# A long convolution by a two-stage Fourier transform beside a diagonal state-space layer, on one core: parity rows in two partition halves, spectra in one layout, and part of the shift convolution on TensorE

## The chip, the cores and the metric

The kernel runs on one core of a Trainium2 chip. The metric is the device time of one execution in microseconds (us). The core's engines work side by side, each through its own instructions in order: TensorE (PE; its weight loads are listed as PEld), VectorE (DVE), ScalarE (ACT), GpSimd (POOL) and SyncE (SP). Transfers are issued from two queues here, SP's and POOL's, and are carried by 16 shared DMA engines.

## The reference

Two independent heads over 2048 time steps and 1024 channels, written side by side into one output of 2048 rows and 2048 columns. All inputs are bf16.

```python
# head A (H3): k, v, q of [2048, 1024]; shift_k [1024, 4]; ssm_k [1024, 2048]; ssm_D [1024]
kv = (causal 4-tap convolution of k along time, with shift_k per channel) * v
y  = (causal convolution of kv along time with ssm_k per channel, by an FFT of length 4096)
a  = q * (y + kv * ssm_D)
# head B (S5): x [2048, 1024], 1024 complex states, diagonal Lam_bar
Bu   = x @ B_bar.T                        # complex
h[t] = Lam_bar * h[t-1] + Bu[t]           # 2048 steps
b    = 2 * real(h @ C.T) + x * Dskip
```

## The kernel before

**Head B** goes in 16 chunks of 128 time steps. For a chunk i, `U.i.*` (line 492) makes 128 matmuls of 128x128 weights `BT` on the transposed chunk `xT`, `ue` copies them out of PSUM on ACT (line 497), then VectorE rotates (`r1`, `r2`: lines 506 and 518), runs the recurrence as a scan (`sc`, line 523), carries the state over (`cm`), and rotates back (`r3`, `r4`: lines 506 and 535). `y.i.*` (lines 546 and 551) multiplies the states by `CT`, 32 matmuls of 512 columns and 8 small ones for the skip term, and `ye` copies that out (line 556). The weights are prepared first: `bl` loads a block of B, `bT` transposes it on TensorE (line 458), `bc` copies it into `BT` (line 473 on ACT, 469 on DVE); C and x come by transposing transfers from SP (`cx`, line 480, and `x`, line 483).

**Head A** is a transform of length 4096, split as 128 x 32. The time steps are cut into 16 residues r ("parity rows"), each a tile of 128 partitions by 1024 channels. VectorE makes kv two residues at a time: `kvm` (line 583, four products), `kva` (597) and `kvb` (602, sums), `kvc` (604, times v), from rows of k loaded by `kp` into a ring `kring`. The first stage multiplies every residue by a constant F1: `am` (line 610) for kv and `hm` (line 643) for the filter, whose transposes are `hl`, `hT` (line 630) and `hc` (635). F1 has 128 rows and 128 columns, of which half are zero, since even and odd rows share the partitions. The results are copied out (`ae` line 615, `he` line 650) and stored to DRAM (`ast`, `hst`). The second stage takes 16 groups gq: `lh` and `lk` load the stored values in another order, `sh` and `sk` (line 676) transform them in 64x64 pieces of the array, `she` (685) and `ske` (691) copy out. Real and imaginary part of a spectrum lie on different partitions; so `sw` makes a swapped copy of the filter's spectrum by four SBUF-to-SBUF transfers for each gq, and `pr` (line 704) multiplies both copies at once. `sa` (line 717) transforms back, `sae` (724) copies out and `vst` stores. The last stage `a3` (line 744) needs, for each residue r, values of all 16 groups: `vl` loads them, `a3e` (749) copies out, `qm` (753) multiplies by q (loaded by `qp`), and `ost` stores.

**Order.** A text, `ORDER`, lists every task in one sequence. Each engine runs its own tasks in that sequence; `@G` and `@S` move a transfer to POOL's or SP's queue, `@D` moves a copy to VectorE, and the letters after a colon name the buffers: `p0`, `p1` are single PSUM banks, `d0` to `d2` pairs of banks, `a` and `b` are rings in SBUF of 4 KB and 2 KB a partition. A task on TensorE that needs an occupied `p` or `d` waits for the copy that empties it.

```python
def s2(key, nm, gq, e, o): ...          # before: one half e of the channels, 64x64 pieces, one pd
def sw(gq):                             # before: four transfers of 32 partitions
    for b in range(4):
        o = b ^ 1
        spd(hab[32 * b:32 * b + 32, 1, :, :], hab[32 * o:32 * o + 32, 0, :, :])
```

Of the kernel before, what the change touches and what calls it, by code (L numbers as in the profile page):

```python
# [70 lines left out]
wb.2:p1 cx.0.1 eo.1 stt.0 wb.0:p0 cx.7.0 wbe.2 stt.1 eo.3 wb.5:p1 bl.3.0:b6 x.1:b2 wbe.5@D wbe.0 stt.3 wb.3:p1 wbe.3 bT.6.1:p0 cx.1.0 dd bT.2.0:p1
kvm.0:m0 vp.1:a1 vp.2:a0 cx.6.0 bc.6.1 cx.6.1 bT.0.1:p0 bc.2.0 bc.0.1@D kp.2@G eo.2 bT.2.1:p1 kva.0 hT.0.0:p0 hc.0.0:b8 stt.2 bc.2.1 hT.0.1:p0
bT.7.1:p1 hc.0.1:b13 kvb.0:a7 bc.7.1 hT.0.6:p0 hm.0.0.1:d0 kvc.0 hc.0.6:b10 hT.0.3:p1 hm.0.0.0:d1 kvm.4:m0 he.0.0.1:b5 am.1.1:d2 hc.0.3:b11
hm.0.6.1:d0 hst.0.0.1 hT.0.2:p0 bT.0.0:p1 he.0.6.1:b8 hc.0.2:b0 hst.0.6.1@S cx.1.1 bc.0.0 bT.7.0:p0 bc.7.0@D cx.3.1 z1 U.0.3.0:p1 kva.4 hm.0.6.0:d0
U.0.3.1 cx.3.0 U.0.2.0:p0 kvb.4:a8 U.0.2.1 ue.0.3:a10 he.0.6.0:b7 kvm.2:m0 bT.1.0:p1 bc.1.0 am.0.1:d0 bT.3.0:p1 ue.0.2 bc.3.0 bT.3.1:p0 bc.3.1
U.0.0.0:p1 U.0.0.1 he.0.0.0:b5 kp.4@G kva.2 kp.3@G ae.0.1:b10 hm.0.3.1:d1 U.2.2.0:p0 ue.0.0 ast.0.1@S vp.4:a5 kvc.4 U.0.1.0:p1 ae.1.1:b4 cx.5.0
hm.0.1.0:d0 he.0.3.1:b6 ast.1.1 kvb.2:a6 hm.0.3.0:d2 hst.0.6.0 U.0.1.1 he.0.1.0:b3 hst.0.3.1 kvc.2 U.2.2.1 ue.0.1 hst.0.1.0 he.0.3.0:b11 U.1.2.0:p1
r1.0:m0 ue.2.2:a0 hst.0.3.0@S hm.0.1.1:d1 hst.0.0.0@S am.4.0:d0 he.0.1.1:b8 cx.2.0 U.2.1.0:p0 r2.0:a1 U.1.2.1 U.2.1.1 ue.1.2:a10 kvm.8:m0 U.1.1.0:p1
ue.2.1 ae.4.0:b13 hm.0.2.0:d2 am.4.1:d1 z2 ast.4.0 am.0.0:d0 U.2.3.0:p0 hst.0.1.1 ae.4.1:b4 U.1.1.1 he.0.2.0:b7 ast.4.1@S sc.0 U.2.3.1 ue.1.1
hst.0.2.0@S hm.0.2.1:d1 cx.7.1 ue.2.3 am.5.1:d2 ae.0.0:b6 hT.0.4:p1 cx.2.1 am.2.0:d0 hc.0.4:b10 ast.0.0 U.1.0.0:p0 ae.2.0:b3 hT.0.7:p1 cx.4.0 kva.8  # L80
U.1.0.1 ue.1.0 hT.0.5:p0 hc.0.7:b0 hl.5:a9 kvb.8:a4 hl.4:a2 U.2.0.0:p1 hc.0.5:b13 ast.2.0@S hl.7:a3 r3.0:m0 U.1.3.0:p0 he.0.2.1:b8 am.1.0:d0 hst.0.2.1
hm.0.5.0:d1 U.1.3.1 cm.0:a7 kvc.8 U.2.0.1 ue.1.3 he.0.5.0:b11 r4.0 U.4.0.0:p0 ue.2.0 hm.0.4.0:d1 r1.1:m0 U.4.0.1 he.0.4.0:b5 U.4.2.0:p1 ue.4.0:a5
# [4 lines left out]
hm.1.4.1:d0 am.9.0:d2 hc.1.3:b9 hst.0.4.1@S ae.9.0:b8 hT.1.5:p0 am.9.1:d1 y.0.1.3 he.1.4.1:b5 r2.4:a5 am.3.1:d2 ye.0.1 hst.1.4.1 hm.1.3.1:d0
y.1.1.0:p1 he.1.3.1:b0 kvm.6:m0 hc.1.5:b3 y.1.1.1 hst.1.3.1@S ae.3.1:b7 hT.1.7:p0 y.1.1.2 ae.9.1:b4 hm.1.4.0:d0 hm.1.5.1:d2 hc.1.7:b10 ast.9.1 y.1.1.3
kp.6 kva.6 hT.1.6:p0 ast.9.0@S ye.1.1:b5 kp.5 hm.1.7.0:d1 hc.1.6:b13 yst.0@S y.1.0.0:p1 ast.3.1@S he.1.5.1:b0 hT.1.1:p0 cm.2:a4 kvb.6:a1 y.1.0.1
hst.1.5.1 hc.1.1:b4 lw.1@G:w0 hm.1.6.0:d2 r3.2:m0 y.1.0.2 he.1.6.0:b2 y.1.0.3 he.1.4.0:b8 hst.1.6.0@S hT.1.0:p0 r4.2 ye.1.0 hst.1.4.0 hm.1.6.1:d2  # L90
hm.1.3.0:d0 he.1.6.1:b13 vp.6@G:a6 U.3.2.0:p1 kvc.6 yst.1 he.1.7.0:b9 hst.1.6.1 hm.1.1.0:d2 kvm.12:m0 U.3.2.1 hc.1.0:b0 hst.1.7.0@S x.7:b11
hm.1.7.1:d1 y.2.0.0:p0 he.1.7.1:b10 x.6:b7 he.1.1.0:b8 y.2.0.1 hm.1.0.0:d1 hst.1.1.0@S hm.1.1.1:d2 he.1.0.0:b2 y.2.0.2 kva.12 ue.3.2:a7 am.6.1:d1
he.1.3.0:b4 U.3.3.0:p1 he.1.1.1:b9 U.3.3.1 kvb.12:a8 hst.1.1.1 hm.1.0.1:d0 ue.3.3 hst.1.0.0 ae.6.1:b5 hT.1.2:p1 kvm.10:m0 y.2.0.3 hc.1.2:b13 ast.6.1
hm.1.5.0:d2 vp.5@G:a2 am.7.0:d1 he.1.0.1:b0 hst.1.7.1 y.2.1.0:p1 ye.2.0:b8 am.7.1:d0 he.1.5.0:b3 y.2.1.1 ae.7.0:b9 kvc.12 kp.7@G hm.1.2.0:d2 y.2.1.2
hst.1.5.0 kva.10 vp.7@G:a9 U.3.1.0:p0 hst.1.3.0 hm.1.2.1:d1 U.3.1.1 he.1.2.1:b2 kvb.10:a10 y.2.1.3 he.1.2.0:b1 hst.1.2.1@S hst.1.0.1@S am.13.1:d1
lw.0:w1 ue.3.1 kvc.10 am.6.0:d2 ae.13.1:b5 U.6.0.0:p0 kvm.14:m0 ae.6.0:b10 am.10.0:d1 ast.13.1@S x.5:b13 U.6.0.1 ye.2.1 ast.6.0 am.10.1:d2 ae.7.1:b3
hst.1.2.0 U.7.3.0:p1 yst.2@S ast.7.0@S ue.6.0:a3 am.12.1:d0 ae.10.0:b2 U.7.3.1 ae.10.1:b4 U.3.0.0:p0 ast.10.0 kva.14 am.12.0:d1 ue.7.3:a6 ast.10.1@S
am.13.0:d2 U.3.0.1 U.6.3.0:p1 ue.3.0 kvb.14:a0 lh.2:a1 ae.13.0:b0 lh.0:a2 U.7.1.0:p0 lh.1:a8 r1.3:m0 ae.12.0:b5 am.11.0:d2 U.6.3.1 ae.11.0:b10
# [725 lines left out]
```

## Time and profile before

| | |
|---|---|
| device time, 3 runs | 379.9, 381.47, 382.37 us; median 381.47 |
| profiled execution, first to last instruction | 378.5 us |
| median less that span | 3.0 us |
| busy: PE, DVE, ACT, POOL | 92%, 86%, 70%, 21% of the span |
| transfers | 100.06 MB, 264 GB/s on average |

The page has the busy time of each engine, the span in 40 slices, the transfers, the chain of work that ended last, and the costliest groups of instructions (line, engine, operation, output <- inputs, shapes, count; busy time and mean length of one; idle time before them and what ended it). A view by stretches of time gives busy time, DMA share and rate. In the chain of work, a row is the start, the length, and what ran. In the view in order of time, a row is the start, the length, the engine, the line, and what was merged. The time of a single matmul in such a row includes the tail in which it drains; the distance between two starts is what it costs.

### The profile page before, as it was taken

The numbers are of one execution on the slowest core, as the hardware profiler recorded it, in microseconds if no ns is written. First come the engines' busy times: TensorE is split into PE (matmuls) and PEld (weight loads), VectorE is DVE, ScalarE is ACT, GpSimd is POOL, SyncE is SP. The second block draws the span as 40 slices with busy tenths as digits, with TensorE's granted clock in tenths as the row PEclk, the third lists the DMA queues.
The fourth block names the chain that finished last, engine by engine and source line by source line (L and its number), as shares of the span: only waits on it lengthen the run. The fifth ranks groups of instructions, "written<-read, shape, count | busy, mean of one in ns | idle before, by whom it ended". The sixth has DMA issues, their size and how long they took to land.

```text
span 378.5 us, 8748 instructions
## 1 busy us (share of the span) xinstructions
PE 346.6 (92%) x3661; PEld 225.6 (60%) x3661; DVE 324.6 (86%) x229; ACT 264.2 (70%) x341; POOL 81.3 (21%) x150
## 2 busy tenths in 40 slices
PE   4548889899899999999999999989999999999995
PEld 3226678785455578855444757367867664467442
DVE  6989599999999997999997797576899999993972
ACT  4978798877778886952785879778869771346433
POOL 7300023022112521214200325330210202211021
PEclk9999999999999999999999999999999999999999
DMA  6999999997578999999999897999989539877995
GB/s 231 317 338 216 265 272 286 296 314 235 200 243 270 247 313 287 281 272 268 190 275 312 258 324 234 220 267 221 284 236 312 175 125 325 306 229 255 350 319 206
DMA packets 67418, 100.06 MB, mean 264 GB/s; under 512 B 38435, under 2 KB 42147, under 8 KB 67380
## 3 DMA queue, kind: packets, MB, share of 16 engines
q1 hardware_dynamic: 54660, 56.32, 54.8%
q0 software_dynamic: 12720, 43.19, 36.8%
q8 instruction: 28, 0.46, 0.5%
q14 instruction: 10, 0.08, 0.1%
HBM read 49.16 MB, written 33.55 MB: 219 GB/s over the span
## 4 chain that ended last, share of the span: by engine, by line
PE 56%; DMA 15%; issue 13%; ACT 7%; SPq 4%; POOL 2%; DVE 1%; POOLq 0%; ACTq 0%; DVEq 0%
PE ps_u L492 22%; PE ps_y L546 16%; PE ps_a L744 4%; DMA wts<-a_c_W 4%; SPq L483 4%; DMA Ys_kv<-ysb 3%; PE ps_a L643 3%; DMA l2k<-Ys_kv 3%; DMA ld<-in_B_B_re_dram 3%; PE ps_a L717 3%; PE ps_a L610 3%; DMA hab<-hab 2%; PE ps_a L676 2%; PE ps_t L630 2%; ACT ysb L615 2%
## 5 line engine op out<-in xcount | busy, mean ns | idle before, releaser
L492 PEld LDWEIGHTS <-BT 128*128 128x128 bf16 x2048 | 119.3, 98 | 22.6 <-issue 11.7
L492 PE MATMUL ps_u<-xT,BT 128*128 128x128 bf16 x2048 | 127.7, 219 | 2.4 <-ACT u L497 1.2
L546 PE MATMUL ps_y<-CT,h 128*128 128x512 bf16 x512 | 127.7, 379 | 0.0
L546 PEld LDWEIGHTS <-h 128*128 128x128 bf16 x512 | 44.6, 98 | 48.0 <-issue 6.1
L523 DVE TENSOR_TENSOR_SCAN h<-rtab,h 128x2080 bf16<-128x2080 f32 x16 | 71.8, 4488 | 0.2
L497 ACT CAST u<-ps_u 128x512 bf16<-128x512 f32 x64 | 38.2, 603 | 27.0 <-PE ps_u L492 19.1
L506 DVE TENSOR_TENSOR mt<-u,Z 128x4096 bf16<-128x4096 bf16 x16 | 36.7, 2291 | 15.8 <-ACT u L497 15.4
L704 DVE TENSOR_TENSOR hab<-x,hab 128x4096 bf16<-128x4096 bf16 x16 | 36.5, 2286 | 15.2 <-DMA hab<-hab 10.5
L556 ACT CAST yo<-ps_y 128x512 bf16<-128x512 f32 x32 | 19.1, 596 | 28.0 <-PE ps_y L546 24.4
L650 ACT CAST ysbh<-ps_a 128x1024 bf16<-128x1024 f32 x32 | 32.3, 1033 | 8.8 <-PE ps_a L643 7.5
L691 ACT CAST x<-ps_a 128x1024 bf16<-128x1024 f32 x32 | 31.9, 1026 | 8.8 <-PE ps_a L676 5.9
L506 DVE TENSOR_TENSOR mt<-h,Z 128x4096 bf16<-128x4096 bf16 x16 | 36.7, 2292 | 0.5
L724 ACT CAST vsb<-ps_a 128x1024 bf16<-128x1024 f32 x32 | 31.7, 1027 | 6.5 <-PE ps_a L717 6.0
L583 DVE TENSOR_TENSOR mt<-kring,wbc 128x2048 bf16<-128x2048 bf16 (+3 forms) x14 | 35.8, 2592 | 0.4 <-ACT wbc L473 0.2
L615 ACT CAST ysb<-ps_a 128x1024 bf16<-128x1024 f32 x32 | 32.3, 1043 | 2.7 <-issue 1.6
L685 ACT CAST hab<-ps_a 128x1024 bf16<-128x1024 f32 x32 | 32.2, 1030 | 2.1 <-PE ps_a L676 1.9
L551 PE MATMUL ps_y<-Dd,xT 128*128 128x128 bf16 x128 | 28.0, 219 | 0.0
L749 ACT CAST ot<-ps_a 128x1024 bf16<-128x1024 f32 x16 | 15.7, 1018 | 14.1 <-PE ps_a L744 14.1
L169 POOL DMA_DIRECT2D Ys_h<-ysbh x20 | 14.3, 716 | 43.3 <-ACT ysbh L650 43.3
L168 POOL DMA_DIRECT2D hab<-hab x32 | 15.6, 494 | 32.1 <-ACT hab L685 18.3
L458 PE MATMUL ps_t<-ident,ld 128*128 128x128 bf16 x128 | 13.9, 285 | 9.1 <-DMA ld<-in_B_B_re_dram 4.4
L643 PE MATMUL ps_a<-hT,F1t 128*128 128x512 bf16 x64 | 20.6, 402 | 0.8 <-ACT ysbh L650 0.6
(116 smaller groups left out, 381.8 us busy)
## 6 DMA issues: line engine op xcount, KB each, us to landing
Ys_h<-ysbh POOLq DMA_DIRECT2D x20, 256.0 KB, 5.5
l2h<-Ys_h SPq DMA_DIRECT2D x9, 512.0 KB, 9.7
Vs<-vsb SPq DMA_DIRECT2D x9, 512.0 KB, 4.3
vv<-Vs SPq DMA_DIRECT2D x9, 512.0 KB, 5.2
Ys_kv<-ysb POOLq DMA_DIRECT2D x17, 256.0 KB, 6.2
l2k<-Ys_kv SPq DMA_DIRECT2D x8, 512.0 KB, 3.9
hab<-hab SPq DMA_DIRECT2D x32, 128.0 KB, 5.4
l2k<-Ys_kv POOLq DMA_DIRECT2D x8, 512.0 KB, 7.8
```

Of the source, the lines that this page charges most:

```text
L492: nc.tensor.matmul(pu[:, w, jl, :], BT[:, 2 * jp + jl, w, d, :], xT[:, d, :], start=(d == 0), stop=(d == ND - 1))
L497: nc.scalar.copy(u[:, :, 2 * jp:2 * jp + 2, :], st["pu", i, jp][:])
L506: nc.vector.tensor_mul(m, s_, w_)
L523: nc.vector.tensor_tensor_scan(gf, rtab[:].rearrange("p a j t -> p (a j t)"), gf, 0.0, ALU.mult, ALU.add)
L546: nc.tensor.matmul(py[:], h[:, 1 - w, j, 2:TP], CT[:, j, w, dh * 512:(dh + 1) * 512], start=(j == 0 and w == 0), stop=(j == NJ - 1 and w = ...
L583: nc.vector.tensor_mul(m[:, :, j0:j0 + n, :], a_, wbc[:, j0:j0 + n, :].unsqueeze(1).to_broadcast([P, 2, n, DV]))
L615: nc.scalar.copy(st["ysb", r, u][:], st["pa", r, u][:].rearrange("p e d -> p (e d)"))
L643: nc.tensor.matmul(pd[:, e, :], F1t[:, u, :], st["hT", f, rp][:, e, :], start=True, stop=not sk)
L650: nc.scalar.copy(st["yh", f, rp, u][:], st["pa", f, rp, u][:])
L685: nc.scalar.copy(hab[:, a, :, e * 512:(e + 1) * 512], st["ps", key, gq, e][:])
L691: nc.scalar.copy(x16[:, :, e * 512:(e + 1) * 512], st["ps", "k", gq, e][:])
L704: nc.vector.tensor_mul(hab, x16.unsqueeze(1).to_broadcast([P, 2, 2 * D]), hab)
```

## The change

1. **Halves.** The parity rows of k, v, q and the output lie as two halves of 64 partitions (`(n h s) d -> h n s d`), each loaded or stored by a transfer of its own: `kp`, `vp`, `qp`, `ost`, `vl` and `hst` issue two transfers where they issued one.
2. **First stage without zeros.** F1 is 64x64; `am` and `hm` make 8 matmuls of 64x64 pieces (four pieces of the array) for each residue in place of 4 of 128x128, into two pairs of banks.
3. **Last stage.** The constant G is 128x64; `a3` makes 4 matmuls in two column halves in place of 4 full ones. `hT` transposes into the same two halves: 16 pieces in place of 8.
4. **Spectra.** `sh` and `sk` make 16 matmuls of 64x32 pieces, and real and imaginary part come to lie on the same partition. `sw` and its 64 transfers are gone; `p1` and `p0`, two products of 2048 elements, replace `pr`, one of 4096. `sa` makes 32 matmuls of 32x64 pieces in place of 16 of 64x64.
5. **Shift convolution.** `NX = 2`: two of the eight blocks of 128 channels are convolved on TensorE. `kx` loads them by two transposing transfers of 2048 rows, `dg` builds diagonal weights, `kt` makes 32 matmuls of 128 columns for two residues, `ke` copies out on ACT. `kvm`, `kva` and `kvb` work on 768 channels, no longer 1024.
6. **Small ones.** The scan runs as two halves with a table half the size; `dg` and `dd` are single products on VectorE.
7. **ORDER** is new as a whole. The whole filter transform (`hT`, `hc`, 11 of 16 `hm`, 20 of 32 `he`) stands ahead of the first `U`; ten of the 16 `bc` are on VectorE up to there; the last `vst` stands later, with 32 parts of `y` and no `U` behind it (45 and 9 before). `kx`, `cx`, `x` and the stores are spread anew over the two queues.

```diff
-NX = 0
+NX = 2
-    kr = k.rearrange("(n s) d -> n s d", s=NR)
+    kr = k.rearrange("(n h s) d -> h n s d", s=NR, h=2)
...
     def kt(r):
-        for b in range(NX):
-            for j in range(4):
-                nc.tensor.matmul(pk[:, b, :], a_, st["dg"][:, b, j, :], start=(j == 0), stop=(j == 3))
+        for e in range(2):
+            for b in range(NX):
+                for j in range(4):
+                    for h in range(2):
+                        nc.tensor.matmul(st["pk", r][64 * h:64 * h + 64, e, b * P:(b + 1) * P], a_, st["dg"][:, b, 3 - j, :],
+                                         start=(j == 0), stop=(j == 3), tile_position=(0, 64 * h))
...
     def sc(i):
-        gf = st["g", i][:].rearrange("p a j t -> p (a j t)")
-        nc.vector.tensor_tensor_scan(gf, rtab[:].rearrange("p a j t -> p (a j t)"), gf, 0.0, ALU.mult, ALU.add)
+        for a in range(2):
+            gf = st["g", i][:, a, :, :].rearrange("p j t -> p (j t)")
+            nc.vector.tensor_tensor_scan(gf, rtab[:].rearrange("p j t -> p (j t)"), gf, 0.0, ALU.mult, ALU.add)
...
-    def am(r, u):
-        pd = dtile("ps_a")
-        for e in range(2):
-            nc.tensor.matmul(pd[:, e, :], F1t[:, u, :], kvt(r)[:, r % 2, e * 512:(e + 1) * 512], start=True, stop=True)
+    def first(pd, src, e, more=()):
+        rows = [src] + list(more)
+        for i, (m, o) in enumerate(rows):
+            for h in range(2 if i == 0 else 1):
+                for u in range(2):
+                    nc.tensor.matmul(pd[64 * u:64 * u + 64, h, :], F1t[64 * h:64 * h + 64, u, :], m[64 * h:64 * h + 64, o],
+                                     start=(i == 0), stop=(i == 1 or h == 1 or len(rows) == 1), tile_position=(64 * h, 64 * u))
+    def am(r):
+        st["pa", r] = [dtile("ps_a") for _ in range(2)]
+        for e in range(2):
+            first(st["pa", r][e], (kvt(r)[:, r % 2, :], slice(e * 512, (e + 1) * 512)), e)
...
-    def s2(key, nm, gq, e, o):
-        for gi in range(2):
-            for u in range(2):
-                nc.tensor.matmul(pd[64 * gi:64 * gi + 64, u, :], wt[up, b0:b0 + 64],
-                                 st[nm, gq][up, gi, e * 512:(e + 1) * 512], start=True, stop=True,
-                                 tile_position=(64 * u, 64 * gi))
+    def s2(key, nm, gq):
+        pd = [dtile("ps_a") for _ in range(2)]
+        for ri in range(2):
+            for j in range(4):
+                for u in range(2):
+                    nc.tensor.matmul(pd[u][32 * j:32 * j + 32, ri, :], wt[up, b0:b0 + 32],
+                                     st[nm, gq][up, j // 2, (j % 2) * 512:(j % 2 + 1) * 512], start=True, stop=True,
+                                     tile_position=(64 * u, 32 * j))
...
-        nc.vector.tensor_mul(hab, x16.unsqueeze(1).to_broadcast([P, 2, 2 * D]), hab)
+        nc.vector.tensor_mul(st["pq", gq][:], st["sk", gq][:], st["sh", gq][:, :, ::-1, :])   # p1
+        nc.vector.tensor_mul(st["sh", gq][:], st["sk", gq][:], st["sh", gq][:])               # p0
...
+        for t, (m, src, ri) in enumerate(((0, "sh", 0), (1, "sh", 1), (2, "pq", 0), (2, "pq", 1))):   # sa
+            for j in range(4):
+                for u in range(2):
+                    nc.tensor.matmul(pd[j // 2][64 * u:64 * u + 64, j % 2, :], wt[jp, b0:b0 + 64],
+                                     st[src, gq][jp, u, ri, :], start=(t == 0), stop=(t == 3),
+                                     tile_position=(32 * j, 64 * u))
...
     def a3_(r):
         for e in range(2):
-            for u in range(2):
-                nc.tensor.matmul(pd[:, e, :], Gt[:, u, :], st["vv", r][:, u, e * 512:(e + 1) * 512], start=(u == 0), stop=(u == 1))
+            for h in range(2):
+                nc.tensor.matmul(pd[64 * h:64 * h + 64, e, :], Gt[:], st["vv", r][:, h, e * 512:(e + 1) * 512], start=True, stop=True,
+                                 tile_position=(0, 64 * h))
```

More of the change, by code (lines that the diff above doesn't have):

```diff
@@ L71 @@
[L71 to L82, printed above, removed]
@@ L87 @@
[L87 to L98, printed above, removed]
@@ new lines @@
+hT.1.4:p0 hm.1.7:d1d2 hc.1.4:b1 kvc.0 vp.2:a4 kt.4:p1 bl.6.1:b5 he.1.5.0:b6 x.0:b2 kvb.6:a5 hT.1.1:p0 ke.4 hc.1.1:b11 kvm.8:m0 kt.6:p1 vp.3:a2 he.1.7.0:b0
+bl.7.1:b3 hT.1.2:p0 ke.6 hm.1.3:d0d1 hc.1.2:b13 hT.1.0:p1 hc.1.0:b10 kvc.4 bT.6.1:p0 kp.6 he.1.7.1:b14 kp.5 U.0.1.0:p1 bc.6.1@D cx.2.1 he.1.3.0:b4 kva.8
+bT.0.1:p0 he.1.3.1:b5 vp.4:a10 hm.1.4:d2d0 U.0.1.1 he.1.4.0:b8 bc.0.1@D hst.1.3.1 kvb.8:a7 hst.1.3.0@S ue.0.1:a8 hm.1.2:d1d2 kvc.6 hst.1.5.0 bT.7.1:p1
+he.1.2.1:b1 U.0.2.0:p0 he.1.2.0:b13 kvm.12:m0 U.0.2.1 bc.7.1 hm.1.6:d2d1 ue.0.2 x.1:b7 U.0.3.0:p1 he.1.4.1:b3 U.0.3.1 vp.6:a4 he.1.6.0:b5 kva.12 U.0.0.0:p0
@@ L144 @@
+a3e.0:b8 ost.14 a3e.11:b13 qm.0 ye.15.1 qm.11 yst.15@S ost.11@S ost.0@S
 """
@@ L571, in vp @@
         st["v", r] = k4("v", [P, 2, D])
-        spd(st["v", r][:], vr[:, 2 * r:2 * r + 2, :])
+        for h in range(2):
+            spd(st["v", r][64 * h:64 * h + 64, :, :], vr[h, :, 2 * r:2 * r + 2, :])
     E["vp"] = vp
@@ L627, in hT @@
         for b in range(4):
-            hv = st["hk", 4 * f + b][:].rearrange("p (n r) -> p r n", r=NR)
+            hv = st["hk", 4 * f + b][:].rearrange("p (n h r) -> p r h n", r=NR, h=2)
             for e in range(2):
-                nc.tensor.transpose(pt[:, e, b * P:(b + 1) * P], hv[:, 2 * rp + e, :], ident[:])
+                for h in range(2):
+                    nc.tensor.matmul(pt[64 * h:64 * h + 64, e, b * P:(b + 1) * P], hv[:, 2 * rp + e, h, :], ident[:],
+                                     is_transpose=True, start=True, stop=True, tile_position=(0, 64 * h))
     E["hT"] = hT
@@ L636, in full_kernel, with hm, he, hst @@
     E["hc"] = hc
-    def hm(f, rp, u):
-        pd = dtile("ps_a")
-        st["pa", f, rp, u] = pd
+    def hm(f, rp):
+        st["pa", f, rp] = [dtile("ps_a") for _ in range(2)]
         for e in range(2):
-            sk = rp == 0 and e == 0
-            nc.tensor.matmul(pd[:, e, :], F1t[:, u, :], st["hT", f, rp][:, e, :], start=True, stop=not sk)
-            if sk:
-                nc.tensor.matmul(pd[:, e, :], F1t[0:1, u, :], st["sd"][0:1, f * HD:(f + 1) * HD], start=False, stop=True)
+            more = [(st["sd"], slice(f * HD, (f + 1) * HD))] if rp == 0 and e == 0 else []
+            first(st["pa", f, rp][e], (st["hT", f, rp][:, e, :], slice(0, HD)), e, more)
     E["hm"] = hm
-    def he(f, rp, u):
-        st["yh", f, rp, u] = k2("ysbh", [P, 2, HD])
-        nc.scalar.copy(st["yh", f, rp, u][:], st["pa", f, rp, u][:])
+    def he(f, rp, e):
+        st["yh", f, rp, e] = k2("ysbh", [P, 2, HD])
+        nc.scalar.copy(st["yh", f, rp, e][:], st["pa", f, rp][e][:])
     E["he"] = he
-    def hst(f, rp, u):
-        gpd(Ys_h[u, 2 * rp:2 * rp + 2, :, f * HD:(f + 1) * HD].rearrange("n k d -> k n d"), st["yh", f, rp, u][:])
+    def hst(f, rp, e):
+        for u in range(2):
+            gpd(Ys_h[u, 2 * rp + e, :, f * HD:(f + 1) * HD].rearrange("(h k) d -> k h d", h=2), st["yh", f, rp, e][64 * u:64 * u + 64, :, :])
     E["hst"] = hst
     def lw(w):
-        st["w", w] = rtile(ring, "w", "wts", [P, 4 * 96 + 2 * 256])
+        st["w", w] = rtile(ring, "w", "wts", [P, 4 * 64 + 2 * 384])
         spd(st["w", w][:], Wv[:, w, :])
@@ L735, in qp @@
         st["qt", r] = k4("qt", [P, 2, D])
[L736 removed]
+        for h in range(2):
+            spd(st["qt", r][64 * h:64 * h + 64, :, :], qr[h, :, 2 * r:2 * r + 2, :])
     E["qp"] = qp
@@ L754, in full_kernel, with ost @@
     E["qm"] = qm
-    E["ost"] = lambda r: gpd(oar[:, r, :], st["ot", r][:])
+    def ost(r):
+        for h in range(2):
+            gpd(oar[h, :, r, :], st["ot", r][64 * h:64 * h + 64, :])
+    E["ost"] = ost
     with tc.manual_schedule():
```

287 lines of the change are left out of this document (135 added, 152 removed).

## The prediction, made before the changed kernel ran

> **What bounds the kernel now.** I read the page first, then the stretches of time, then the chain of work, and last single rows in order of time.
>
> ```profile
> span 378.5 us, 8748 instructions
> ...
> PE 346.6 (92%) x3661; PEld 225.6 (60%) x3661; DVE 324.6 (86%) x229; ACT 264.2 (70%) x341; POOL 81.3 (21%) x150
> ...
> DMA packets 67418, 100.06 MB, mean 264 GB/s; under 512 B 38435, under 2 KB 42147, under 8 KB 67380
> ...
> PE 56%; DMA 15%; issue 13%; ACT 7%; SPq 4%; POOL 2%; DVE 1%; POOLq 0%; ACTq 0%; DVEq 0%
> ```
>
> TensorE is busy 92% of the span and holds most of the chain; VectorE follows closely. The stretches show where TensorE is not the bound (columns: busy PE, PEld, DVE, ACT, POOL, clock, DMA share, GB/s).
>
> ```profile
> 0.00:10.00 10.00, 4.11 (x33) 3.34 (x33) 6.97 (x22) 5.17 (x6) 7.11 (x19) 1.00 0.69 237
> 10.00:20.00 10.00, 5.36 (x22) 2.32 (x23) 9.43 (x29) 9.09 (x18) 3.45 (x7) 1.00 1.05 310
> 20.00:30.00 10.00, 5.05 (x37) 3.63 (x37) 8.26 (x12) 7.69 (x21) 0.53 (x1) 1.00 1.15 339
> 30.00:40.00 10.00, 8.72 (x50) 5.10 (x49) 9.53 (x10) 6.88 (x8) 0.74 (x1) 1.00 1.08 219
> ...
> 340.00:360.00 20.00, 20.00 (x164) 11.93 (x163) 13.57 (x12) 10.57 (x14) 1.13 (x2) 1.00 0.86 299
> ```
>
> For 30 us TensorE is half idle while VectorE and the DMA engines are nearly full; later it is full, as in the last row. So the span is a sum: the time of the first `U`, what TensorE has left at that moment, its waits, and the tail.
>
> ```profile
> 44.11 1.05 PE ps_u L492 x16
> ...
> 45.60 2.68 PE ps_u L492 x48
> 48.28 0.46 PE ps_t L458 x8
> ...
> 55.82 0.86 PE ps_a L643 x4
> 56.69 2.68 PE ps_u L492 x48
> ```
> ```profile
> 87.13 1.84 ACT ysb L615 x2
> ...
> 370.98 3.68 PE ps_y L546 x17
> ```
>
> The first `U` is at 44.1 us. A 128-column matmul costs 2.68/48 = 0.056 us, eight transposes 0.46, four 512-column matmuls 0.86, so one 0.216 (3.68/17 says the same); a copy of 1024 columns on ACT, back to back, 0.92. The last matmul ends at 374.7; 3.8 us of copy and store follow.
>
> **What small pieces cost.** TensorE alone, in order of time:
>
> ```profile
> 206.78 1.06 PE L492 MATMUL ps_u<-xT,BT 128*128 128x128 bf16 x16
> 207.77 1.06 PE L717 MATMUL ps_a<-hab,wts 64*64 64x512 bf16 x16
> 208.66 0.39 PE L676 MATMUL ps_a<-l2h,wts 64*64 64x512 bf16 x4
> 208.98 1.24 PE L492 MATMUL ps_u<-xT,BT 128*128 128x128 bf16 x19
> ```
>
> Sixteen 64x64 matmuls take 208.66 - 207.77 = 0.89 us, four rounds of 0.22: the four pieces work at once, and a round costs what one full matmul costs. But the four from 208.66 hold the engine 0.32 us until full-array work starts, and the 16 `U` from 206.78 take 0.99 where 16 x 0.056 is 0.895: entering or leaving the pieces costs about 0.1 us each way (I use 0.093). Full-size first stages have no such gap: 55.82 + 0.86 runs straight into the `U` at 56.69.
>
> **TensorE from the first U on, before.** `U` 128 x 0.895 = 114.6; `y` 128 x 0.864 plus 128 small ones of 0.056, 117.8; `am` and `hm` 60 x 0.43 = 25.8; 11 `hT` and 3 `bT` 14 x 0.46 = 6.4; `sh` and `sk` 64 x 0.216 = 13.8; `sa` 32 x 0.43 = 13.8; `a3` 16 x 0.86 = 13.8: 306.0. The order changes between full array and pieces 78 times: 7.3. From 44.1 to 374.7 are 330.6, so 17.3 us are waits, 3.4 of them around `hT`, which moves away:
>
> ```profile
> L630 PE MATMUL ps_t<-ident,hk 128*128 128x128 bf16 x128 | 12.5, 252 | 3.4 <-ACT hT L635 1.9 <-ACT yo L556 0.7 <-ACT u L497 0.7
> ```
>
> **The same, after.** `U` and `y` stay: 232.4. `am`, 15 left, 8 matmuls in two rounds, 0.43 each: 6.5; `hm`, 5 left: 2.2. `kt`, 4 left, 16 rounds of two column halves of 0.056: 3.6. Two `bT`: 0.9. `sh` and `sk`, 16 matmuls in two rounds of eight pieces: 32 x 0.43 = 13.8, as before; `sa`, 32 matmuls in four rounds: 13.8, as before; `a3`, two rounds of two halves: 6.9. Sum 280.1. No row shows eight pieces or column halves at work. The nearest, the 64x64 round, says one round each, and I take it; with only four at a time `sh`, `sk` and `sa` take 27.6 more; below a round nothing goes, since each piece streams 512 columns. The new order changes the kind of piece 191 times, 157 of them after the first `U`: 14.6. So TensorE's remainder falls from 313.3 to 294.7, by 18.6.
>
> [...]
>
> **The first U, after.** Here the gain goes. The whole filter transform and more of kv now stand ahead of it.
>
> ```profile
> L583 DVE TENSOR_TENSOR mt<-kring,wbc 128x2048 bf16<-128x2048 bf16 (+3 forms) x14 | 35.8, 2592 | 0.4 <-ACT wbc L473 0.2
> ...
> L597 DVE TENSOR_TENSOR mt<-mt 128x4096 bf16<-128x4096 bf16 x8 | 18.3, 2285 | 0.1
> L753 DVE TENSOR_TENSOR ot<-ot,qt 128x1024 bf16<-128x1024 bf16 x16 | 10.2, 686 | 3.4 <-ACT ot L749 2.7 <-DMA qt<-in_A_q_dram 0.7
> L602 DVE TENSOR_TENSOR acc<-mt 128x2048 bf16<-128x2048 bf16 x8 | 9.8, 1224 | 0.8 <-PE ps_t L630 0.5
> ...
> L469 DVE CAST wbc<-ps_a 128x512 bf16<-128x512 f32 x4 | 2.7, 688 | 0.4 <-PE ps_a L409 0.3
> ...
> L469 DVE COPY BT<-ps_t 128x1024 bf16<-128x1024 bf16 x2 | 1.4, 692 | 5.8 <-PE ps_t L458 5.8
> ```
>
> ACT: 41 wide copies (20 `he`, 16 `hc`, 2 `ae`, 3 `bc`) for 18 (11 `bc`, 5 `hc`, 2 `he`): 23 x 0.92 = +21.2; five half copies more (`ke`, `wbe`) and the eight small ones of `dd` gone, about even. TensorE has three pairs of banks and two single ones to fill, so it can't run ahead of ACT. VectorE: five `kvm` of 3.4 (35.8/8 x 0.75) for two of 4.5, +8.0; four `kva` of 1.7 for one of 2.3, +4.5; four `kvb` of 0.9 for one of 1.2, +2.4; two more `kvc`, as long as a `kvb` of before, +2.4; ten `bc` for two, +5.5; three `wbe` fewer, -2.1; `dg` and `dd` at 0.69, the nearest product of 1024, +1.4 (twice that if the broadcast slows them): +22.1. Bytes: the new order issues about 20 MB ahead of the first `U`, the old one 14; 6 MB at 289 GB/s, the mean from 10 to 40 us, are 20.8. The three agree: 44.1 + 21 to 22 = **66 us**. The ends: 62, where the three overlap better than before, and 75, where SP's queue is blocked. `kx.0` and `kx.1` are transposing transfers on SP, and this is the only row for such an issue:
>
> ```profile
> L483 SPq DMA_TRANSPOSE xT<-in_B_x_dram x16: 1242/1972/8410, 7.0 to 252.8; - x16
> ```
>
> Behind `kx.1` stand five `hst` issued from SP, which free the buffers that `he` and `hc` write: if a `kx`, twice as long, holds SP twice 8.4 us, ACT runs out of buffers, then TensorE of banks.
>
> **The rest.** VectorE loses a quarter of 63.9 (16.0) and gains 2.5 by `p1` and `p0` (1.22 each for one of 2.29), 5.5 by `bc` and little by the split scan (0 to 0.3 each, a small instruction's length): about 318 busy in place of 324.6, so it does not become the bound. The swaps go:
>
> ```profile
> hab<-hab SPq DMA_DIRECT2D x32, 128.0 KB, 5.4
> ```
>
> That is 64 x 128 KB, 8.4 of 100 MB, and 5.4 us in each group's chain; TensorE hardly waited for it, so I book nothing (0 to 5 us of the waits). Halved transfers issue one more each: 225 from SP for 187, 127 from POOL for 138, off the path except at the end, where four stores of `ost` follow the last `yst`. At 0.32 each:
>
> ```profile
> L169 SPq DMA_DIRECT2D Vs<-vsb x9: 319/320/540, 192.5 to 311.2; - x9
> ```
>
> +1.3. **Sum:** 66 + 294.7 + 13.9 (waits) + 3.8 + 1.3 = 379.7 us of span, 378.5 before; with the 3.0 us by which the median exceeds the span, **382.7**.
>
> **The rivals.** (1) *The waits shrink* (faster). Fewer bytes and no swaps leave TensorE 6 us of waits, and the first `U` comes at 63: 368.8, so 371.8 us. For it speaks the DMA share above 1 up to 40 us; against it that few waits of TensorE name a transfer. (2) *The end is bound by transfers* (slower). No `vl` can start before the last `vst`, since each reads all groups. Before, that was at 311.2, and 18.4 MB (`vl`, `qp`, `ost`, `yst`) had 67 us: 273 GB/s. Now 32 parts of `y` and 16 `a3` are left, 38 us of TensorE with the changes, 43 with the tail, for 14.4 MB: 335 GB/s. It decides if the rate stays below that: at 299, the stretch from 340 us, +5; at 273, +10; I price +8: 391. Against it: that stretch had a share of 0.86, so 348 at a full share, and my sum books 0. (3) *The pieces don't run eight wide*, so that the smaller tiles don't do what they are for: +27.6, 410.
>
> **How the numbers follow.** Forecast 0.36, with 377 to 388 as its own range; rival 1 0.34, rival 2 0.24, rival 3 0.06. About 1% is what a measurement of this kernel tells from no change, 377.7 to 385.3. Faster: 0.34 and 0.06 of the forecast's lower edge, 0.40. Slower: 0.24, 0.06 and 0.05 of its upper edge, 0.35. Same: 0.25. The range, 367 to 397, leaves out rival 3, the first `U` at 75 together with rival 2, and a start below 62 with almost no waits.
>
> **What would show it.** The first `U` between 62 and 70 us, with ACT and VectorE over 80% busy until then; starts 0.216 apart from round to round in `sh`, `sk`, `sa`, with eight matmuls a round, and `a3` at half its 0.86; gaps of 0.1 us around every group of pieces; after the last `vst`, TensorE without a gap over 1 us (right) or waits for `vv` (rival 2). I am wrong if the first `U` is as early as before, or if the waits after it are under 8 or over 25 us.

## The result and the profile after

The changed kernel takes 420.41 us (median of four runs, 418.02 to 424.42), the kernel before 381.92 (379.9 to 383.05): a ratio of 1.0988, 95% interval 1.0898 to 1.1079. It is slower by a tenth, where 382.7 was predicted. One of the four executions, 424.42 us, was slow against the others, and the ratios, here and below, leave such executions out. The page of its profiled execution (418.02 us, span 416.3):

```profile
span 416.3 us, 10820 instructions
...
PE 360.8 (87%) x4683; PEld 234.2 (56%) x4683; DVE 316.8 (76%) x272; ACT 258.9 (62%) x332; POOL 74.5 (18%) x139
...
DMA packets 73102, 91.74 MB, mean 220 GB/s; under 512 B 43394, under 2 KB 50830, under 8 KB 73054
...
PE 51%; DMA 17%; SPq 11%; ACT 3%; issue 2%; DVE 1%; POOL 0%; ACTq 0%; POOLq 0%
```

Fewer bytes than before (91.74 MB for 100.06) went at a lower rate (220 GB/s for 264), VectorE and ScalarE are less busy, and TensorE's share fell. So no engine became the bound. The stretches of time, with the columns as before (busy PE, PEld, DVE, ACT, POOL, clock, DMA share, GB/s), show where TensorE stood still:

```profile
20.00:30.00 10.00, 8.09 (x115) 6.26 (x117) 3.30 (x9) 7.44 (x11) 0.55 (x1) 1.00 1.20 192
30.00:40.00 10.00, 6.47 (x84) 4.53 (x82) 9.93 (x9) 10.00 (x18) 2.95 (x6) 0.66 1.09 289
...
100.00:120.00 20.00, 17.56 (x260) 14.46 (x258) 19.90 (x14) 12.34 (x16) 0.46 (x1) 0.91 1.08 204
120.00:140.00 20.00, 16.63 (x164) 9.86 (x161) 9.52 (x6) 8.31 (x11) 5.95 (x10) 0.91 0.94 243
340.00:360.00 20.00, 20.00 (x200) 8.99 (x200) 16.55 (x12) 11.04 (x14) 1.08 (x2) 1.00 0.98 287
360.00:380.00 20.00, 15.78 (x93) 6.27 (x92) 4.35 (x6) 9.09 (x11) 6.96 (x12) 1.00 1.05 235
380.00:400.00 20.00, 15.62 (x73) 5.97 (x72) 4.57 (x7) 5.47 (x8) 4.73 (x10) 0.74 1.00 314
```

From 360 to 380 us, in the last stage, the DMA share is full at 235 GB/s, where the row of 340 to 360 us before had 299 at a share of 0.86. Full engines that move less: by share and rate, 2 KB took 146 ns of one of the 16 engines (16 x 1.05 / 235 GB/s), and 94 before (16 x 0.86 / 299). The granted clock, 1.00 before, falls to 0.66 to 0.91 in four of these rows. The chain of work in the tail (with two pairs of equal matmuls, early and late, to show what the clock does), what TensorE waited for in the last stage, and the first `U` in order of time on TensorE:

```profile
341.55 0.43 PE ps_y L529 x2
...
351.55 4.63 DMA Vs<-vsb
...
358.27 4.95 DMA vv<-Vs
...
367.63 7.65 DMA vv<-Vs
375.29 14.94 DMA vv<-Vs
390.36 1.08 PE ps_a L731 x4
...
394.62 0.85 PE ps_y L529 x2
```
```profile
PE ps_a L731 <- DMA vv<-Vs: 7.8, 7, 2.1
```
```profile
72.04 1.05 PE L474 MATMUL ps_u<-xT,BT 128*128 128x128 bf16 x16 [0.60 <-ACT hT L632]
```

Three loads of `vv` stand in the chain with 27 us, and TensorE waited for `vv` seven times, 7.8 us in all and 2.1 the longest. At 394.62 us two matmuls of 512 columns took 0.85 us, where at 341.55 they took 0.43: TensorE ran there at half speed, and the clock granted from 390 to 395 us was 0.50. By the prediction's steps, in the profiled executions: the first `U` at 72.0 for 66; from there to the last `vst` 279.5 for 270.6 in the sum (294.7 + 13.9, less the 38 that stand behind it); from the last `vst` to the end 64.7 for 43.1. Together 36.6.

### The profile page after: what moved, and what is told of

It reads as the page before. It is cut to its first block, busy times and chain, and to the rows that moved or that the text cites. A ratio compares the mean times of both kernels' runs of the same rounds, so it can differ in the third digit from the quotient of the medians.

```text
span 416.3 us, 10820 instructions
## 1 busy us (share of the span) xinstructions
PE 360.8 (87%) x4683; PEld 234.2 (56%) x4683; DVE 316.8 (76%) x272; ACT 258.9 (62%) x332; POOL 74.5 (18%) x139
## 2 busy tenths in 40 slices
DMA packets 73102, 91.74 MB, mean 220 GB/s; under 512 B 43394, under 2 KB 50830, under 8 KB 73054
## 4 chain that ended last, share of the span: by engine, by line
PE 51%; DMA 17%; SPq 11%; ACT 3%; issue 2%; DVE 1%; POOL 0%; ACTq 0%; POOLq 0%
PE ps_y L529 19%; PE ps_u L474 17%; DMA vv<-Vs 7%; SPq L462 5%; PE ps_a L672 4%; SPq L154 4%; PE ps_a L702 3%; DMA wts<-a_c_W 3%; DMA Ys_h<-ysbh 2%; DMA CT<-in_B_C_re_dram 2%; PE ps_k L422 2%; SPq L465 2%; PE ps_y L534 1%; PE ps_t L626 1%; PE ps_a L596 1%
## 5 line engine op out<-in xcount | busy, mean ns | idle before, releaser
L474 PE MATMUL ps_u<-xT,BT 128*128 128x128 bf16 x2048 | 124.8, 220 | 0.9 <-ACT hT L632 0.6
L680 ACT CAST s<-ps_a 128x1024 bf16<-128x1024 f32 x64 | 62.6, 1020 | 19.6 <-PE ps_a L672 18.8
L506 DVE TENSOR_TENSOR_SCAN h<-rtab,h 128x1040 bf16<-128x1040 f32 x32 | 72.5, 2309 | 0.2
L488 DVE TENSOR_TENSOR mt<-u,Z 128x4096 bf16<-128x4096 bf16 x16 | 36.6, 2290 | 6.1 <-ACT u L479 5.9
L488 DVE TENSOR_TENSOR mt<-h,Z 128x4096 bf16<-128x4096 bf16 x16 | 36.6, 2288 | 0.2
L741 DVE TENSOR_TENSOR ot<-ot,qt 128x1024 bf16<-128x1024 bf16 x16 | 10.7, 690 | 34.0 <-ACT ot L737 32.2
L686 DVE TENSOR_TENSOR pq<-s,s 128x2048 bf16<-128x2048 bf16 x16 | 19.5, 1221 | 13.3 <-ACT s L680 11.4
L568 DVE TENSOR_TENSOR mt<-kring,wbc 128x1536 bf16<-128x1536 bf16 (+3 forms) x14 | 28.0, 2033 | 2.0 <-DMA kring<-in_A_k_dram 1.9
L626 PE MATMUL ps_t<-ident,hk 128*64 128x128 bf16 x256 | 16.8, 293 | 10.8 <-DMA hk<-in_A_ssm_k_dram 7.7
L154 POOL DMA_DIRECT2D Ys_kv<-ysb x15 | 9.1, 608 | 80.6 <-ACT ysb L607 78.5
L626 PEld LDWEIGHTS <-hk 128*64 128x64 bf16 x256 | 15.7, 203 | 12.3 <-DMA hk<-in_A_ssm_k_dram 8.3
L500 DVE TENSOR_TENSOR h<-mt 128x2048 bf16<-128x2048 bf16 x16 | 19.6, 1224 | 1.5 <-PE ps_y L529 1.0
```

Source lines behind the costliest of these rows:

```text
L474: nc.tensor.matmul(pu[:, w, jl, :], BT[:, 2 * jp + jl, w, d, :], xT[:, d, :], start=(d == 0), stop=(d == ND - 1))
L488: nc.vector.tensor_mul(m, s_, w_)
L506: nc.vector.tensor_tensor_scan(gf, rtab[:].rearrange("p j t -> p (j t)"), gf, 0.0, ALU.mult, ALU.add)
L568: nc.vector.tensor_mul(m[:, :, j0:j0 + n, :], a_, wbc[:, j0:j0 + n, :].unsqueeze(1).to_broadcast([P, 2, n, DV]))
L626: nc.tensor.matmul(pt[64 * h:64 * h + 64, e, b * P:(b + 1) * P], hv[:, 2 * rp + e, h, :], ident[:], is_transpose=True, start=True, stop=Tr ...
L680: nc.scalar.copy(s16[:, u, :, :], st["ps", key, gq][u][:])
```

## The experiments

**H** says that the halved transfers cost the time, **O** that the order does. The columns after the ratio are of the profiled execution: first `U`, last `vst`, end. The runs were made in three groups (whole to nx0, wp to cols, mix to n3), and beside each group the kernel before was measured again: medians of 380.4, 380.1 and 378.7 us, single executions from 373 to 389. The changed kernel was measured only once, beside 381.9. So a difference of a few us between two groups, or between a group and the changed kernel, is not safe.

| run | median us | ratio to before, 95% | first U | last vst | end |
|---|---|---|---|---|---|
| after | 420.4 | 1.099 [1.090, 1.108] | 72.0 | 351.6 | 416.3 |
| whole | 395.0 | 1.044 [1.033, 1.055] | 68.6 | 338.9 | 393.1 |
| last | 412.3 | none; 406.0, 408.5, 416.2, 417.5 us | 72.7 | 349.8 | 404.3 |
| first | 402.7 | 1.062 [1.047, 1.077] | 66.2 | 336.4 | 397.3 |
| nx0 | 421.7 | 1.118 [1.105, 1.132] | 77.1 | 354.5 | 419.4 |
| wp | 408.5 | 1.081 [1.058, 1.104] | 69.7 | 342.7 | 402.2 |
| wf | 394.4 | 1.047 [1.033, 1.061] | 66.8 | 337.1 | 392.0 |
| twoq | 413.3 | 1.098 [1.082, 1.113] | 76.6 | 352.3 | 411.6 |
| cols | 401.8 | 1.067 [1.054, 1.080] | 70.9 | 345.5 | 400.5 |
| mix | 391.3 | 1.039 [1.029, 1.049] | 70.9 | 342.0 | 392.1 |
| spec | 397.6 | 1.052 [1.038, 1.067] | 42.9 | 329.0 | 396.0 |
| m3 | 399.6 | 1.060 [1.050, 1.071] | 69.3 | 342.5 | 400.2 |
| n3 | 399.8 | 1.057 [1.044, 1.070] | 67.0 | 337.5 | 398.5 |

### Which part

**whole** undoes parts 1 to 3 in the new order (the arrays in DRAM have the same layout either way):

```diff
-        for u in range(2):
-            spd(st["vv", r][64 * u:64 * u + 64, :, :], Vs[u, r, :, :].rearrange("(h k) d -> k h d", h=2))
+        spd(st["vv", r][:], Vs[:, r, :, :].rearrange("u k d -> k u d"))
...
```

In the same way `kp`, `vp`, `qp`, `hst`, `ast` and `ost` are whole, `am`, `hm` and `a3` use the 128x128 constants, and `hT` and `kt` go in full width.

> The changed kernel with parts 1 to 3 undone: parity rows whole in the partitions again, so every kp, vp, qp, hst, ast, vl and ost is one transfer of 128 partitions, am and hm are four full matmuls, a3 four full ones, hT and kt full width. Order, spectra (sh, sk, p1, p0, sa) and the shift convolution on TensorE stay. Theory H (the halved transfers cost the time: 0.57 to 0.62 us of SP's time for each half against 0.36 for a whole one, and packets of 2 KB that take 140 ns against 94 in the tail): the first U back by 3 or more, the tail from the last vst to the end from 64.7 to about 50 us, in all 390 to 402 us of device time, although the full matmuls cost TensorE about 9 us more. Theory O (the order: only 32 parts of y behind the last vst, 14 MB to move meanwhile, whatever the shape of the transfers): the tail stays at 60 to 68 us, and the total at 412 to 428.

**last** and **first** undo one stage each.

> The changed kernel with the last stage alone undone (vl, qp and ost whole, a3 four full matmuls); the first stage stays in halves. Theory H: the tail falls by 10 to 15 us, the front stays at 72: 404 to 411 us. Theory O: 415 to 424.

> The changed kernel with the first stage alone undone (kp, vp, hst, ast whole; am, hm, hT, kt full width); vl, qp and ost stay in halves. Theory H: the first U 3 to 6 us sooner and the stalls of 100 to 140 us gone, the tail as slow as with the change (63 to 66): 405 to 414 us. Theory O: 416 to 425, as the full first stages cost TensorE some 5 us more.

**nx0** sets `NX = 0` and drops `kx`, `dg`, `kt` and `ke`.

> The changed kernel with part 5 alone undone: the shift convolution wholly on VectorE again (1024 channels in kvm, kva, kvb; no kx, dg, kt, ke), halves and spectra as changed. Theory K (the two transposing transfers of kx, 9.8 and 4.3 us on SP's queue, and kt with slow weights make the first U late): the first U from 72 to 66 us or sooner, 409 to 415 us of device time. If kx and kt are hidden, VectorE's extra products (a third more in kvm, kva and kvb) make it 420 to 430 us.

Whole transfers took back 25.4 us, with (by the expectation) 9 us more of full matmuls to do. The tail is 54.2 us in run whole (393.1 - 338.9) for 64.7: H, not O. Both stages pay: undoing the first took back 17.7, the last about 8 by the medians and 12 by the profiled executions. Run first came out below H's 405 to 414 us, and run last, whose executions scatter, just above its 404 to 411; whether the two effects add up, these runs do not show. The last stage's effect lies in the tail (54.5 in run last, 60.9 in run first), the first stage's ahead of it. In nx0 the first `U` came later, not sooner, with VectorE (third busy column) full up to it:

```profile
40.00:60.00 20.00, 9.46 (x82) 4.10 (x74) 19.90 (x23) 17.04 (x22) 9.18 (x16) 0.50 0.95 264
60.00:80.00 20.00, 16.84 (x214) 13.30 (x215) 19.93 (x14) 14.97 (x17) 2.96 (x5) 0.83 1.09 266
```

So theory K fell, and the time lies in the range for extra products on VectorE. Part 5 gives no gain when it is undone; whether it is worth a per cent or two, the ratios (1.118 and 1.099, with intervals that overlap) do not decide.

### Number of transfers, or partitions

**wp** and **wf** start from run whole and cut `kp`, `vp`, `qp`, `hst` and `vl` in two, by partition or by row:

```diff
+        for p in range(2):        # wp
+            spd(st["vv", r][64 * p:64 * p + 64, :, :], Vs[:, r, 64 * p:64 * p + 64, :].rearrange("u k d -> k u d"))
+        for u in range(2):        # wf
+            spd(st["vv", r][:, u, :], Vs[u, r, :, :])
```

> The kernel of run whole (parts 1 to 3 undone), in which kp, vp, qp, hst and vl are each cut again into two transfers of 64 partitions, 0 to 63 and 64 to 127; nothing else changes, no matmul and no copy. [...] Theory N (the number of transfers and SP's time to issue them): also slower, 403 to 420 us, but with packets near 100 ns, and no slower than run wf.

> The kernel of run whole, in which the same kp, vp, qp, hst and vl are cut into two transfers of all 128 partitions each, by row instead of by partition: as many transfers and bytes as in run wp, and the same packets. [...] Theory N: as slow as run wp, 403 to 420.

The stretch in which the `vl` run, in after, whole, wp and wf; then the transfers by kind of wp and of wf, with their number, size and median us from issue to landing:

```profile
356.00:391.00 35.00, 27.20 (x153) 11.39 (x152) 10.87 (x13) 11.81 (x14) 9.95 (x18) 0.96 1.02 255
```
```profile
342.00:373.00 31.00, 30.64 (x160) 14.45 (x159) 12.19 (x13) 11.74 (x14) 5.80 (x9) 1.00 0.95 322
```
```profile
347.00:381.00 34.00, 29.76 (x152) 13.84 (x154) 11.02 (x13) 11.97 (x15) 8.16 (x14) 1.00 1.02 255
```
```profile
341.00:371.00 30.00, 29.84 (x155) 14.31 (x157) 11.39 (x13) 12.03 (x15) 7.47 (x14) 1.00 0.92 325
```
```profile
vv<-Vs SPq DMA_DIRECT2D x22, 256.0 KB, 8.2
```
```profile
vv<-Vs SPq DMA_DIRECT2D x22, 256.0 KB, 4.3
```

As many transfers of the same bytes, for `vl` in the same packets of 2 KB: cut by row they cost nothing against run whole, cut by partition 14 us (408.5 for 394.4). With 64 partitions the engines are full at 255 GB/s (share 1.02), as in the changed kernel; with 128 they are not full at 325 (0.92). By share and rate, 2 KB took 131 ns of one of the 16 engines in wp and 93 in wf, on average over the stretch. Theory N fell. The issue of a half is longer too (shortest, median and longest ns of an issue, then when), and the last run below shows that this does not decide; after and run wf, SP's `vl`:

```profile
L153 SPq DMA_DIRECT2D vv<-Vs x22: 573/605/625, 356.3 to 391.3; - x22
```
```profile
L157 SPq DMA_DIRECT2D vv<-Vs x22: 319/424/877, 341.1 to 371.5; - x22
```

### Two queues

**twoq** sends the two halves of a pair from SP and POOL:

```diff
+    dq = lambda h: (nc.sync if h == 0 else nc.gpsimd).dma_start
-            spd(st["vv", r][64 * u:64 * u + 64, :, :], ...)
+            dq(u)(st["vv", r][64 * u:64 * u + 64, :, :], ...)
```

> The changed kernel with the two halves of each kp, vp, qp, hst, ast, vl and ost on two queues, the first half from SP and the second from POOL, where both stood on one; bytes, shapes, matmuls and order of tasks stay. [...] Theory N: SP's own list shortens by the halves that leave it, POOL's grows, so the front gains 2 to 4 us and the packets stay at 125 or more: 412 to 420.

413.3 us for 420.4, but the same ratio to the kernel before (1.098 and 1.099). The time lies in theory N's range, but the front did not gain: the first `U` came at 76.6, later than with the change, and it was the tail that shortened, to 59.2 us. The rate of the `vl` stretch was 250 GB/s at a share of 0.97 (127 ns for 2 KB), for 255 with both halves on one queue and 322 in run whole.

### Column halves

**cols** puts `hT` and `kt` alone back into column halves:

```diff
-    a_ = bass.AP(kv_.tensor, kv_.offset + o, [list(kv_.ap[0]), [16, P]])
+    for h in range(2):      # o + 1024 * h, into partitions 64 * h
+        a_ = bass.AP(kv_.tensor, kv_.offset + o, [list(kv_.ap[0]), [16, 64]])
```

> The kernel of run whole with hT and kt alone in two column halves of 64 again (their 16 and 32 matmuls in place of 8 and 16; rows of time in whole order). Theory W (column halves load their weights at half speed: 0.12 us a round of kt against 0.056, 1.12 us for an hT against 0.46): four kt behind the first U cost 4 us, and 15 hT and 4 kt ahead of it cost 14 us of TensorE's time, of which idle time there hides most: 398 to 404 us. If the rounds themselves cost nothing more than full ones: 394 to 396.

It cost 6.8 us, as theory W says: 2.3 up to the first `U` and 4.3 from there to the last `vst` (274.6 for 270.3). Weight loads by line and shape: the 64 columns of `kT` in run cols, then all 128 of them in run whole; then `kt` in full width in run whole, in order of time:

```profile
L426 PEld LDWEIGHTS <-kT 128*64 128x64 bf16 x256 | 16.0, 217 | 2.4 <-issue 2.3
```
```profile
L425 PEld LDWEIGHTS <-kT 128*128 128x128 bf16 x128 | 9.9, 151 | 1.9 <-issue 1.4
```
```profile
62.41 1.36 PE L425 MATMUL ps_k<-dg,kT 128*128 128x128 bf16 x16
63.61 0.66 PE L619 MATMUL ps_t<-ident,hk 128*128 128x128 bf16 x8
```

A `kt` takes 63.61 - 62.41 = 1.20 us in full width and about 1.93 in halves, although the halves stream at once (in the changed kernel's trace, by the median, the two matmuls of a round start 8 ns apart, the rounds 111 ns). Half the columns of `kT` take 217 ns to load where all of them took 151.

### The change without its half transfers

**mix** keeps all the small matmuls and replaces every half transfer by a whole one of the same bytes. The rows then lie in other partitions than the transform needs, so this run is for its time alone:

```diff
-        for h in range(2):
-            spd(st["qt", r][64 * h:64 * h + 64, :, :], qr[h, :, 2 * r:2 * r + 2, :])
+        spd(st["qt", r][:], qr[:, 2 * r:2 * r + 2, :])      # rows land elsewhere
...
```

> The changed kernel with all its matmuls, copies and its order, but every transfer of 64 partitions replaced by one of 128 that moves the same bytes (kp, vp, qp, hst, vl, ost once instead of twice, ast as often); rows so land in other places than the mathematics wants, and the output is not the reference's. It gives the time of the change without its half transfers. Theory S (the sum of the prediction held but for the half transfers and the column halves' weights): run whole less the full matmuls of first and last stage (15.5 us), plus 61 more changes of mode (5.7) and the column halves of run cols (6.8): 392, taken as 386 to 397. Theory T (the transfers explain only what runs wp and last showed, some 14 to 17 us, and the small matmuls cost more than summed): 401 to 408.

The stretch of its `vl`:

```profile
346.00:373.00 27.00, 26.58 (x157) 11.75 (x156) 11.01 (x13) 11.71 (x14) 5.79 (x9) 1.00 0.96 349
```

Theory S: 391.3 for 392. So the half transfers cost 29 us by the medians (420.4 - 391.3), and 24 by the profiled executions (416.3 - 392.1): 1.1 up to the first `U`, 8.4 from there to the last `vst`, 14.6 behind it. The ratios (1.099 and 1.039) make it 0.060 x 382 = 23. The two medians are of different groups, so I take 23 to 29. Part of this may come through the clock: its mean was 0.954 in the changed kernel and 0.964 in run mix (1.000 before), so an estimate of what was withheld is 0.046 x 416.3 = 19 us and 0.036 x 392.1 = 14, a difference of at most 5.

### Part 4 by itself

**spec** is the kernel before with the new spectra; since `sh`, `sk` and `sa` take two pairs of banks at once, their tasks move back in the old order:

```diff
-sh.7.0:d1
...
-she.7.0:e0
...
-sh.7.1:d0
...
-she.7.1
-sw.7
...
-pr.7
+sh.7:d1d0
+she.7.0:e0
...
+she.7.1
...
+p1.7
+p0.7
```

> The kernel before with part 4 alone: spectra with real and imaginary part on one partition, no swapping transfers, p1 and p0 in place of pr, and the scan in two halves with the small table to make room. Its order is the old one; sh, sk and sa, which now take both pairs of banks at once, stand where their second half stood, and tasks that this blocks are moved back as little as the banks allow. By the sum TensorE has the same rounds as before, and it is busy 92% of the span there, so all that can go are waits: 372 to 383 us. If the pairs of banks, taken two at a time, make TensorE wait for the copies: 384 to 395.

Slower than either guess. Two of TensorE's waits in it, which name the copies that empty the banks:

```profile
PE ps_a L670 <- ACT vsb L710: 4.7, 6, 1.0
...
PE ps_a L670 <- ACT hab L682: 2.8, 3, 0.9
```

The kernel before has no such waits, 7.5 us in all. So part 4 needs an order of its own; what it would be worth in one is open.

### Which partitions

**m3** and **n3** cut each `vl` of run whole in three:

```diff
+        for a, b in ((0, 32), (32, 96), (96, 128)):    # m3; n3: ((0, 32), (32, 64), (64, 128))
+            spd(st["vv", r][a:b, :, :], Vs[:, r, a:b, :].rearrange("u k d -> k u d"))
```

> The kernel of run whole with each vl in three transfers: partitions 0 to 31, 32 to 95 and 96 to 127. The middle one has 64 partitions, half of them below and half above partition 64. [...] Theory Q (any transfer of fewer than 128 partitions is slow): as n3.

> The kernel of run whole with each vl in three transfers: partitions 0 to 31, 32 to 63 and 64 to 127; as many pieces of the same sizes as in run m3. [...] Theory Q: as m3.

```profile
346.00:380.00 34.00, 31.11 (x160) 14.27 (x159) 11.83 (x13) 12.06 (x15) 10.57 (x19) 1.00 1.03 264
```
```profile
341.00:375.00 34.00, 29.55 (x153) 13.62 (x151) 11.86 (x13) 11.74 (x14) 10.68 (x19) 1.00 1.02 270
```

No difference (m3 first; 399.6 and 399.8 us), as theory Q says; if the side of partition 64 is what counts, m3 should have been the faster. But half of the bytes in m3 still went in pieces of 32 partitions of one side. So the last run measured the transfers alone.

**probe**: no computation, 16 transfers of 256 KB a phase.

```python
half = (64 * (i % 2), 64 * (i % 2) + 64)
parts = {"all": (0, 128), "low": (0, 64), "mid": (32, 96), "alt": half, "two": half}   # two: odd i from POOL
```

> Transfers by themselves: no part of the computation is left, only five phases of 16 loads of 256 KB in pieces of 2 KB (run twice over), then five of 16 stores; each phase waits for the one before. In a phase the loads go to all 128 partitions, to 0-63 alone, to 32-95 alone, to 0-63 and 64-127 in turn from SP, or in turn from SP and POOL. [...] Theory Q (any 64 partitions are slow): 32-95 as slow as 0-63. Theory R (the load of the rest of the kernel, not the partitions, made the packets slow): all phases within 10% of each other.

Stretches inside the five phases of loads (all, low, mid, alt, two), then of stores in the same order; the columns are busy DVE and POOL, clock, DMA share, GB/s:

```profile
19.00:31.00 12.00, 0.00 (x0) 0.00 (x0) 1.00 1.01 345
34.00:54.00 20.00, 0.00 (x0) 0.00 (x0) 1.00 1.03 209
57.00:69.50 12.50, 0.00 (x0) 0.00 (x0) 1.00 0.96 335
72.00:90.00 18.00, 0.00 (x0) 0.00 (x0) 1.00 1.04 233
92.50:108.50 16.00, 0.00 (x0) 3.74 (x7) 1.00 1.00 262
202.00:213.00 11.00, 0.00 (x0) 0.00 (x0) 1.00 0.99 367
215.00:235.00 20.00, 0.00 (x0) 0.00 (x0) 1.00 0.96 208
238.00:249.00 11.00, 0.00 (x0) 0.00 (x0) 1.00 0.96 363
251.00:267.00 16.00, 0.00 (x0) 0.00 (x0) 1.00 0.85 262
269.00:284.00 15.00, 0.00 (x0) 3.54 (x6) 1.00 0.99 274
```

Theories Q and R fell. Partitions 32 to 95 are nearly as fast as all 128 (335 for 345 GB/s), 0 to 63 go at 209, and the two halves in turn, which is what the changed kernel does, at 233 from one queue and 262 from two. Stores are alike (367, 208, 363, 262, 274). So it is not 64 partitions at a time that are slow, as theory Q says, but 64 that lie on one side of partition 64. In the loads to 0 to 63 the engines were full at 209 GB/s (share 1.03): they did not stand idle for want of issues, so the issue time isn't the cause either. Why the side counts, no run shows, nor why two queues don't give the full rate, nor why m3 gained nothing over n3.

## Why the prediction was wrong, step by step

- **Halved transfers: the step that failed.** The prediction booked them as "one more" issue each, "off the path except at the end", +1.3 us. They cost 23 to 29. It counted issues and bytes, and took the rate of the end from rows in which the transfers had 128 partitions; the runs showed that with 64 on one side they go slower (wp and wf, 255 GB/s for 325; probe, 209 for 335). Even the price of an issue was that of a whole store (0.32 us); a half takes 0.573 to 0.625.
- **Rival 2 was the right mechanism and too small.** The end was bound by transfers, whose rate stayed below the 335 GB/s that it asked for; why the rate would be so low it did not say. It was priced +8, "348 at a full share" speaking against it. With halves a full share is 255. From the last `vst` on it came to +21.6. With whole transfers the row of mix says 349, and TensorE had 26.6 busy us of 27: the argument would have held, though the time from the last `vst` to the end is 50.1 us even there, for 43.1 in the sum.
- **The first `U`: within its range, and late.** 72.0 for 66, in the range of 62 to 75. The half transfers account for little of it: 70.9 in run mix. The column halves account for 2.3 (cols against whole), and 68.6 in run whole still is 2.6 late, which stays open. The shift comes with the new order: in run spec, which has the old one, it is at 42.9. The named danger, that `kx` holds SP's queue and leaves ACT without buffers, did not come about: up to the first `U` the changed kernel's trace lists no wait of ACT for a store.
- **Rounds and changes of mode: right.** The 157 changes are in the trace (187 in all, where 191 were counted). Groups of 16 (`sh`), and 8 and 32 matmuls, as the change has them:

```profile
176.34 0.56 PE ps_a L672 x16
...
227.83 1.00 PE ps_a L702 x32
```

  Two rounds of eight pieces by the sum 0.43 + 0.093 = 0.52, four rounds 0.86 + 0.093 = 0.95. So rival 3 (four at a time, +27.6) is out.
- **`kt` and `hT`: mis-sized.** 16 rounds of 0.056 were 0.90 us and measured 1.93, so 4.1 us over the four `kt` behind the first `U`, and 6.8 in all in run cols. The sum took a round of column halves at the 0.056 of a full matmul; the weights of half the columns of `kT` took 217 ns to load there, those of all the columns in run whole 151.
- **Waits.** In mix, from the first `U` to the start of the last matmul are 312.2 us; the sum gives 308.6, with 4.1 for `kt` 312.7. The 13.9 of waits hold there, as a total. In the changed kernel the same way is 331.6. The sum has no term for the clock, and takes it as 1.00.
- **VectorE:** 316.8 us busy for about 318, and not the bound.

In sum: 382.7, plus 6.8 for the column halves, is 389.5, and run mix, which has them and no half transfers, took 391.3; the rest up to 420.4 is the half transfers. That the two agree to 2 us is in part luck. By the ratio mix is 3.9% slower than the kernel before, where 389.5 is 2.1% above the 381.5 that the prediction started from. And the profiled execution of mix is 12.4 us above the sum (392.1 for 379.7): 4.9 at the first `U`, 3.6 on the way to the last matmul, 3.9 behind it. The column halves are 6.8 of that; the remainder, the clock perhaps, stays open. That the kernel is not faster even without the half transfers is, by the sum, the first `U`, which gives back the gain on TensorE; no version run here beats the kernel before.

## What to carry to other kernels

Saving matmul rounds by putting data into 64-partition halves changes the transfers too: check what partitions each DMA touches before counting its bytes, since 0-63 and 64-127 in turn ran at 233 to 262 GB/s where 128 partitions, or 32-95, ran at 335 to 345. Splitting a transfer along the row instead cost nothing here (394.4 us for 395.0). A full DMA share at a low rate in the stretches of time (1.02 at 255 GB/s, where whole transfers had 0.95 at 322) is the sign to look for.

## What the runs showed of the hardware that was not expected

- Stores from 0-63 are as slow as loads to them (208 and 209 GB/s), stores from 32-95 as fast as from all (363 and 367).
- By share and rate, 2 KB took 96 ns of one of the 16 engines at 128 partitions and 161 at 0-63 alone (loads in run probe: 1.01 at 345 GB/s, 1.03 at 209).
- Going over to pieces of 64x32, 32x64 or 128x64 cost the same 0.093 us as to 64x64 (medians in the changed kernel's trace); coming back cost 0.12 to 0.14: two rounds held TensorE 0.555 to 0.559 us for 0.43, four 1.002 for 0.864.
- The granted clock, 1.00 in the profiled execution before, fell to 0.66 to 0.91 over stretches of 10 to 20 us, and equal matmuls then took twice as long (0.85 us for 0.43). Around 388 us this follows waits for `vv` (2.1 us up to 386.9, 1.5 up to 390.4); from 30 to 40 us TensorE waited for copies of ACT (1.8 and 1.7). What lowers the clock, no run shows.
